# Float64 weights in two VectorE steps behind a ScalarE step, small masks in PSUM, and a new order, in a fused attention and two-layer kernel

## The chip, the cores and the metric

The kernel runs on one core of one Trainium2 chip, in one launch. The metric is device time in microseconds (us) of that core. A program written in Python builds the whole instruction stream ahead of time: every engine (TensorE or PE, VectorE or DVE, ScalarE or ACT, GpSimd or POOL, and SyncE or SP, which issues all the transfers) then runs its own list in order, with semaphores between the engines.

## The reference

Three stages follow each other. Attention takes q, k and v in float32 (2 batches, 8 heads, 768 positions, 64 wide); each query and key is assigned to the nearest of 16 centroids of its head, and only pairs with the same cluster count. Then come two dense layers on 1536 tokens, 512 to 2048 to 512 wide, with float64 weights:

```python
q_assign = np.argmax(np.einsum('bhsd,hcd->bhsc', q_n, c_n), axis=-1)
k_assign = np.argmax(np.einsum('bhsd,hcd->bhsc', k_n, c_n), axis=-1)
mask = q_assign[:, :, :, None] == k_assign[:, :, None, :]
scores = np.where(mask, scale * np.matmul(q, k.transpose(0, 1, 3, 2)), -1000000000.0)
attn = np.exp(scores - np.max(scores, axis=-1, keepdims=True))
attn = attn / (np.sum(attn, axis=-1, keepdims=True) + 1e-09)
x = np.matmul(attn, v)            # heads side by side: 1536 x 512
h = x @ w_in;  x2 = (h * np.cos(h)) @ w_out                         # layer 1
h = x2 @ w_in; out = (h * (1.0 / (1.0 + np.exp(-h)))) @ w_out       # layer 2, other weights
```

## The kernel before

Every matrix product is made of three f16 products: each operand is scaled by a power of two and split into a high part (the value rounded to f16) and a low part (the rest). So nearly every piece of data goes through a rounding to f16 (ScalarE as a rule) and a subtraction (GpSimd or VectorE) before TensorE can use it.

**Weights.** Each of the four weight matrices is loaded in 16 pieces of 128 by 512 float64, as pairs of 32-bit words, into a buffer of 4 KB a partition (`conv`, load on line 692). VectorE builds the float32 bit pattern from the upper word by shifts and masks (L698 and L701, or L704 and L706) and ors in the upper bits of the lower word (L713 or L716). In 20 of the 64 pieces (`LOW`: 8 of the first w_in, 4 of each other matrix) the third step is instead a ScalarE conversion of the lower word (L710) and an addition on GpSimd (L711). `VIA` says for which matrices the half-made word lies in one of three PSUM buffers (`p_pb`, which the scores and the layer-1 products use too): all but layer 2's w_out. A sum over the weights follows, on TensorE (`gram`) for layer 1 and on ScalarE (L438) for layer 2, then a power-of-two scale and the split into high and low (`split`, L753 or L754, L737 to L741, L765).

**Attention.** K and V of a pair of heads are loaded, scaled, split and transposed (`prep_kv`); Q likewise for two blocks of 128 queries (`prep_q`). `clusters` finds the largest of 16 products with centroids by five small VectorE steps (L548 to L556) and writes the cluster's mask into extra columns, so that a wrong cluster lowers the score. `attention` takes a block of 128 queries, head by head in order: scores on TensorE (L905), the row maximum on VectorE (L915), exponentials on ScalarE (L934) with their sum, rounding (L941 on ScalarE or L943 on VectorE), the low part on GpSimd (L948), a transposing DMA (L514), and the product with V (L958). At the end of a block the sums are inverted (L967 to L969), the result is scaled, split and transposed into `xT`.

**Layers.** `layer1_in` (L1034 to L1036) and `layer1_out` (L1092 to L1094) run for units of one or two blocks, mixed with the attention of later units. After the last attention the right half of the memory is reused for layer 2's weights; `layer2` (from L1113) then runs in three parts of 512 tokens.

**Order.** No order is written by hand. Each step is a task with an engine, a planned duration, dependences, buffers and a priority; `Graph.run` plays the plan forward and takes, on each engine, the ready task with the lowest priority number whose buffers are free. The instruction streams are issued in that planned order. The table `T` holds the offsets of the priorities and, for tasks that may run on either of two engines (`alt`), a handicap in planned microseconds for the second. `DLAT` is the planned latency of a transposing DMA beyond its length.

Of the kernel before, what the change touches and what calls it, by code (L numbers as in the profile page):

```python
# [21 lines left out]
T = dict(PW_IN=-684337, PW_OUT=-449, PW_STEP=418, W_AHEAD=-1995, KV0=823, KSTEP0=-2590, V0=926, Q0=-836, KSTEP=558, PREP=-1693,  # L22
         PREPQ=1972, LD=-1140, LOB=0.16, WB=-2.45, HB=0.96, EB=10.85, KB=-9.17, GB=2.58, CB=0.17, XB=-0.43, SB=1.07, L2B=-1018,
         PV=-1572, HI=16965, LO=957, XP=2026, G1=3179, GE=531, GC=1965, G2=4172, GO=147, W2=-641, XD=94557, TB=7.8, WH=-0.35,
         GATE=0)
UNITS = [(0, 0, 1), (0, 1, 1), (0, 2, 2), (0, 4, 2), (1, 0, 2), (1, 2, 2), (1, 4, 2)]

LOW = (2,1,1,1)
# [90 lines left out]
class Graph:  # L119
# [9 lines left out]
    def add(self, eng, dur, fn, deps=(), pri=0.0, acq=(), use=(), lat=0.0, table=None, alt=None, port=False):  # L129

        opts = {eng: (dur, fn, 0.0)}
        if alt:
            opts[alt[0]] = (alt[1], alt[2], alt[3])
# [103 lines left out]
def dve(cols, fast=False):  # L237
    return 0.069 + cols / (1920 if fast else 960)
# [30 lines left out]
DLAT, LLAT, SLAT = 1.18, 1.7, 0.3  # L269


def fused_kernel(tc, q, k, v, cent, w1i, w1o, w2i, w2o, out, dbg=None):
# [4 lines left out]
    P = 128  # L277
# [24 lines left out]
    with tc.manual_schedule(), tc.tile_pool(name="dram", bufs=1, space=DRAM) as dpool:  # L302
# [45 lines left out]
        ohb = rsb([P, 4 * NT * NC + 8 * NT], F16, "ohb")  # L348
# [179 lines left out]
        def clusters(nb, stacks, rhs, dst, dep, pr, use, psum_use):  # L528
# [29 lines left out]
            t = add("DVE", 3 * dve(nb * NC) + 0.17, f_o2, [t], pr, use=[oh], port=True)  # L558
# [23 lines left out]
        def prep_kv(b, hp, pr):  # L582
# [17 lines left out]
                      [sc], pr, acq=[nk], use=[kf, ring])  # L600
            lo_k = lo_task(hk, lambda: nk.ap[:, :, :, 0:64], lambda: kf.ap, lambda: c(2), n, [h_k], [nk, kf, ring], pr, PRE[0][b])
            c_k = add("DVE", dve(n / 2, True), lambda: DV.tensor_copy(na.ap[:, :, :, 32:96], hk()), [h_k], pr + 5, acq=[na], use=[nk],
                      alt=("ACT", act(n), lambda: AC.activation(out=na.ap[:, :, :, 32:96], in_=hk(), func=AF.Copy), T["CB"]), port=True)
# [23 lines left out]
            t = add("ACT", act(n, SCL), lambda: AC.activation(out=vb.ap[:, 0], in_=vf.ap, func=AF.Copy, scale=vs), [t], pr, acq=[vb], use=[vf])  # L627
# [4 lines left out]
        def prep_q(b, t, pr):  # L632
# [3 lines left out]
            if t % 2 == 0:  # L636
# [8 lines left out]
                sg_t = add("DVE", 0.13, lambda: DV.tensor_scalar(  # L645
# [8 lines left out]
                      [sc], pr, acq=[nq], use=[qf2, ring])  # L654
            lo_q = lo_task(hq, lambda: nq.ap[:, 0, :, 64:128], qv, lambda: c(2), n, [h_q], [nq, qf2, ring], pr, PRE[1][b])
            c_q = add("DVE", dve(n / 2, True), lambda: DV.tensor_copy(nq.ap[:, 1, :, 32:96], hq()), [h_q], pr + 5, use=[nq],
                      alt=("ACT", act(n), lambda: AC.activation(out=nq.ap[:, 1, :, 32:96], in_=hq(), func=AF.Copy), T["CB"]), port=True)
# [12 lines left out]
        def x_scale(b):  # L670

            m, xi, fac = col(), col(), col(NPAIR)
# [3 lines left out]
            def f():  # L676
                DV.tensor_reduce(out=m, in_=sv[b], axis=AX.X, op=ALU.min)
                DV.tensor_reduce(out=xi, in_=svi[b], axis=AX.X, op=ALU.max)
                DV.tensor_scalar(fac, svi[b], m, None, op0=ALU.mult)
# [5 lines left out]
        def conv(dst, acc, src, shape3, pri, dst_buf=None, pool=None, deps=(), dst_deps=(), add_low=False, via=False):  # L685
# [5 lines left out]
            d = lambda: dst().bitcast(I32)  # L691
            l = add("SP", dma(P * WC * 8), lambda: SP.dma_start(out=wi(), in_=src), deps, pri - T["W_AHEAD"], acq=[w], lat=LLAT)
            ex = [dst_buf] if dst_buf else []
            if via:

                mb = Buf(p_pb)
                m = lambda: mb.ap[:, :WC].bitcast(I32)
                a = add("DVE", dve(WC), lambda: DV.tensor_scalar(  # L698
                    m(), word(1), 3, 0x3FFFFFFF, op0=ALU.logical_shift_left, op1=ALU.bitwise_and), [l], pri, acq=[mb], use=[w])
                to, td, tu = (d, dst_deps, ex) if add_low else (m, (), [])  # L700
                b_ = add("DVE", dve(WC), lambda: DV.scalar_tensor_tensor(  # L701
                    to(), word(1), -0x40000000, m(), op0=ALU.bitwise_and, op1=ALU.bitwise_or), [a, *td], pri - 1, acq=tu, use=[w, mb])
            else:
                a = add("DVE", dve(WC, True), lambda: DV.tensor_scalar(  # L704
                    d(), word(1), 3, 0x3FFFFFFF, op0=ALU.logical_shift_left, op1=ALU.bitwise_and), [l, *dst_deps], pri, acq=ex, use=[w], port=True)
                b_ = add("DVE", dve(WC), lambda: DV.scalar_tensor_tensor(  # L706
                    d(), word(1), -0x40000000, d(), op0=ALU.bitwise_and, op1=ALU.bitwise_or), [a], pri - 1, use=[w, *ex], port=True)
            if add_low:

# [627 lines left out]
```

## Time and profile before

| | us |
|---|---|
| three timed runs | 802.25, 803.54, 804.64 |
| median | 803.54 |
| the profiled execution, its own time | 802.85 |
| its span, first to last instruction | 800.5 |
| busy in it: PE, DVE, ACT, POOL | 711.9, 533.2, 493.5, 282.9 |

The span is what the profile sees; the own time of the same execution holds 2.35 us more around it. Busy times are unions over an engine's instructions, so an engine that is never idle has the whole stretch as its busy time. Durations of single instructions overlap with their neighbours on the same engine.

### The profile page before, as it was taken

Reading aid. Unit: us, or ns where it says so; the run is one execution under the profiler, and the core shown is the slowest. Engines: PE = TensorE matmul, PEld = TensorE weight load, DVE = VectorE, ACT = ScalarE, POOL = GpSimd, SP = SyncE. Lnnn points to the kernel's source line nnn. Section 1 sums busy time; section 2 is a strip of 40 time slices with the busy share of each in tenths; the row PEclk is TensorE's granted clock in tenths of the full one; section 3 lists DMA queues with packets and bytes.
Section 4 is the critical chain, followed back from the end, with each engine's and each line's share of the span. In section 5 each row is a group of like instructions: output and inputs, shape, how many; then the busy total and the mean of one; then the engine's idle time right before and its main releaser. Section 6 shows DMA issues by size and latency. Waiting matters only on the chain.

```text
span 800.5 us, 16869 instructions
## 1 busy us (share of the span) xinstructions
PE 711.9 (89%) x6745; PEld 485.4 (61%) x6745; DVE 533.2 (67%) x1151; ACT 493.5 (62%) x773; POOL 282.9 (35%) x240
## 2 busy tenths in 40 slices
PE   2468777988978998999999999999899999999998
PEld 1344354867956977877887888884344444444443
DVE  7899798697778798798688757787970155015400
ACT  4658676798888898889678755555671254015400
POOL 3242455367676366557458532241020000000000
PEclk9999689999998999999999999999999999999999
DMA  8944399969999999979969965432041000000000
GB/s 305 330 158 133 85 206 208 210 113 211 184 200 193 248 186 189 188 162 209 206 141 193 194 200 202 145 119 67 27 137 73 27 1 0 27 27 1 0 27 26
DMA packets 233902, 111.29 MB, mean 139 GB/s; under 512 B 199520, under 2 KB 221536, under 8 KB 233824
## 3 DMA queue, kind: packets, MB, share of 16 engines
q1 hardware_dynamic: 233824, 110.23, 62.0%
q8 instruction: 52, 0.85, 0.4%
q14 instruction: 26, 0.21, 0.1%
HBM read 50.36 MB, written 10.49 MB: 76 GB/s over the span
## 4 chain that ended last, share of the span: by engine, by line
PE 52%; DVE 19%; DMA 14%; issue 6%; ACT 4%; POOL 4%; SPq 0%; POOLq 0%; DVEq 0%; ACTq 0%
DMA gen<-gen 8%; PE pb L1217 4%; PE pb L1219 4%; PE pb L1218 4%; DMA ws<-in_moe_w_in_dram 4%; PE pb L905 4%; PE xn_ps L958 3%; POOL gen L948 3%; PE pb L1034 3%; PE pb L1036 3%; PE pb L1035 3%; PE xn_ps L1254 3%; PE xn_ps L1252 3%; PE xn_ps L1253 3%; PE g_ps L1254 3%
## 5 line engine op out<-in xcount | busy, mean ns | idle before, releaser
L948 POOL TENSOR_TENSOR gen<-e,gen 128x768 f16<-128x768 f32 x96 | 159.2, 1671 | 64.2 <-ACT gen L941 34.8
L1034 PE MATMUL pb<-xT,w 128*128 128x256 f16 (+1 forms) x448 | 110.8, 260 | 4.6 <-DVE cols L443 4.6
L1036 PE MATMUL pb<-xT,w 128*128 128x256 f16 (+1 forms) x448 | 111.0, 260 | 0.0
L1035 PE MATMUL pb<-xT,w 128*128 128x256 f16 (+1 forms) x448 | 110.8, 260 | 0.0
L934 ACT ACTIVATE e<-pb,small 128x768 f32<-128x768 f32 x96 | 94.6, 988 | 26.3 <-DVE small L919 10.8
L1093 PE MATMUL g_ps<-gT,w 128*128 128x256 f16 (+1 forms) x448 | 109.7, 257 | 0.7 <-POOL gT L1058 0.7
L1094 PE MATMUL g_ps<-gT,w 128*128 128x256 f16 (+1 forms) x448 | 109.8, 257 | 0.0
L1092 PE MATMUL g_ps<-gT,w 128*128 128x256 f16 (+1 forms) x448 | 109.7, 257 | 0.0
L915 DVE TENSOR_REDUCE small<-pb 128x1 f32<-128x768 f32 x96 | 89.7, 950 | 12.6 <-PE pb L905 12.3
L905 PE MATMUL pb<-kst,qst 96*128 96x512 f16 (+3 forms) x384 | 79.4, 339 | 10.6 <-DVE w L713 2.6
L958 PE MATMUL xn_ps<-vst,gen 128*128 128x64 f16 x1728 | 67.8, 196 | 21.3 <-DMA gen<-gen 21.3
L958 PEld LDWEIGHTS <-gen 128*128 128x128 f16 x1728 | 62.1, 100 | 34.9 <-DMA gen<-gen 30.7
L1058 POOL TENSOR_TENSOR gT<-e,gT 128x768 f16<-128x768 f32 (+2 forms) x36 | 54.7, 1529 | 77.3 <-ACT gT L1057 55.2
L1217 PE MATMUL pb<-x2T,w 128*128 128x512 f16 x192 | 73.4, 382 | 2.6 <-DVE e L1233 2.6
L1219 PE MATMUL pb<-x2T,w 128*128 128x512 f16 x192 | 73.5, 383 | 0.0
L1218 PE MATMUL pb<-x2T,w 128*128 128x512 f16 x192 | 73.4, 382 | 0.0
L941 ACT ACTIVATE gen<-e 128x768 f16<-128x768 f32 x86 | 71.0, 839 | 1.2 <-PE xn_ps L958 0.9
L1233 DVE SCALAR_TENSOR_TENSOR e<-e,pb 128x512 f32<-128x512 f32 x48 | 32.9, 685 | 57.8 <-ACT e L1231 57.7
L1237 DVE SCALAR_TENSOR_TENSOR w<-e,w 128x512 f16<-128x512 f32 x48 | 33.5, 700 | 50.2 <-PE pb L1219 27.1
L905 PEld LDWEIGHTS <-qst 128*128 128x128 f16 (+1 forms) x384 | 36.7, 101 | 34.1 <-issue 16.6
L1092 PEld LDWEIGHTS <-w 128*128 128x128 f16 x448 | 43.7, 98 | 9.6 <-issue 1.7
L1035 PEld LDWEIGHTS <-w 128*128 128x128 f16 x448 | 44.3, 99 | 8.5 <-issue 4.9
(201 smaller groups left out, 1520.7 us busy)
## 6 DMA issues: line engine op xcount, KB each, us to landing
ws<-in_moe_w_out_dram SPq DMA_DIRECT2D x24, 512.0 KB, 4.6
gT<-in_moe_w_in_dram SPq DMA_DIRECT2D x16, 512.0 KB, 4.8
ws<-in_moe_w_in_dram SPq DMA_DIRECT2D x16, 512.0 KB, 4.1
xT<-in_moe_w_out_dram SPq DMA_DIRECT2D x8, 512.0 KB, 4.8
w_dram<-x2s SPq DMA_DIRECT2D x16, 256.0 KB, 2.8
st<-w_dram SPq DMA_DIRECT2D x8, 512.0 KB, 3.5
stq<-in_q_dram SPq DMA_DIRECT2D x6, 512.0 KB, 5.0
gen<-in_k_dram SPq DMA_DIRECT2D x8, 384.0 KB, 5.3
```

The source lines that it names most:

```text
L905: PE.matmul(out=sbk.ap[:, c0:c1], lhsT=qs.ap[:kk, a, h], rhs=kb.ap[:kk, a, j].rearrange("p t c -> p (t c)")[:, c0:c1], start=(a == 1), sto ...
L948: tl = add("POOL", pool2(S), lambda hi=hi, lo=lo, ex=ex: PO.tensor_tensor(lo(), ex(), hi(), op=ALU.subtract), [th], pr + T["LO"], use=[*eu ...
L958: PE.matmul(out=o, lhsT=hb.ap[:, pi, kt], rhs=vb.ap[:, vi, j, kt], start=(kt == 0 and pi == 0 and vi == 0), stop=(kt == NT - 1 and pi == 1 ...
L1034: PE.matmul(out=o, lhsT=wh[:, d, fs], rhs=xb.ap[:, 0, d, :n], start=(d == 0), stop=False)
L1035: PE.matmul(out=o, lhsT=wh[:, d, fs], rhs=xb.ap[:, 1, d, :n], start=False, stop=False)
L1036: PE.matmul(out=o, lhsT=wl[:, d, fs], rhs=xb.ap[:, 0, d, :n], start=False, stop=(d == ND - 1))
L1092: PE.matmul(out=o, lhsT=wh, rhs=gh, start=(f == 0 and i == 0), stop=False, skip_group_check=True)
L1093: PE.matmul(out=o, lhsT=wh, rhs=gl, start=False, stop=False, skip_group_check=True)
L1094: PE.matmul(out=o, lhsT=wl, rhs=gh, start=False, stop=(f == NF - 1), skip_group_check=True)
L1217: PE.matmul(out=o, lhsT=wh[:, d, fs], rhs=x[:, 0, d], start=(d == 0), stop=False)
L1218: PE.matmul(out=o, lhsT=wh[:, d, fs], rhs=x[:, 1, d], start=False, stop=False)
L1219: PE.matmul(out=o, lhsT=wl[:, d, fs], rhs=x[:, 0, d], start=False, stop=(d == ND - 1))
```

## The change

- `conv` has one form for all 64 pieces. ScalarE turns the lower word into a float32 near -2 whose lowest mantissa bits are the lower word's upper bits and whose top bits are set; VectorE shifts the upper word and ors it in; VectorE puts the top two bits right with an or and an and. The half-made word lies in PSUM where `VIA` says so, else in place of the lower word. `LOW` is gone.
- `clusters` writes its masks as float32 into unused columns of the same PSUM buffer instead of f16 in memory.
- The roundings of K, V, Q and their copies, of the exponentials and of layer 1's result may run on any of three engines, each with its own handicap.
- The sums of a block are prepared on GpSimd (two steps) and inverted on VectorE; one scale of Q's moves to GpSimd; the maxima of layer 1's result are kept in one array and reduced once.
- `DLAT` goes from 1.18 to 2.24, and every number of `T` is new, so that the order of all tasks differs. Layer 1's w_in keeps a priority far in front; K and V of the last two head pairs now come before it (`KSTEP0`), and the loads of weights are moved in front of where they stood (`W_AHEAD`).

```diff
-T = dict(PW_IN=-684337, PW_OUT=-449, PW_STEP=418, W_AHEAD=-1995, KV0=823, KSTEP0=-2590, V0=926, Q0=-836, KSTEP=558, PREP=-1693,
...
+T = dict(PW_IN=-4283839, PW_OUT=-527, PW_STEP=702, W_AHEAD=1200, KV0=-1591, KSTEP0=-2793319, V0=4033, Q0=-668, KSTEP=313,
...
-LOW = (2,1,1,1)
...
-DLAT, LLAT, SLAT = 1.18, 1.7, 0.3
+DLAT, LLAT, SLAT = 2.24, 1.7, 0.3
...
-                DV.tensor_tensor(e2(), e1(), io, op=ALU.mult)
-                DV.tensor_reduce(out=m2(), in_=e2(), axis=AX.X, op=ALU.max)
-                DV.tensor_tensor(e1(), io, m2().to_broadcast(bc), op=ALU.is_equal)
+                DV.tensor_tensor(pv(2), pv(1), io, op=ALU.mult)
+                DV.tensor_reduce(out=m2(), in_=pv(2), axis=AX.X, op=ALU.max)
+                DV.tensor_tensor(e1(), pv(2), m2().to_broadcast(bc), op=ALU.is_equal)
...
             h_k = add("ACT", act(n, SCL), lambda: AC.activation(out=hk(), in_=kf.ap, func=AF.Copy, scale=c(2)),
-                      [sc], pr, acq=[nk], use=[kf, ring])
+                      [sc], pr, acq=[nk], use=[kf, ring],
+                      alt=[("POOL", pool1(n), lambda: PO.tensor_scalar(hk(), kf.ap, c(2), 1.0, op0=ALU.mult, op1=ALU.mult), T["KP"]),
+                              ("DVE", dve(n, True), lambda: DV.tensor_scalar(hk(), kf.ap, c(2), None, op0=ALU.mult), T["KD"])], port=True)
...
-                a = add("DVE", dve(WC), lambda: DV.tensor_scalar(
-                    m(), word(1), 3, 0x3FFFFFFF, op0=ALU.logical_shift_left, op1=ALU.bitwise_and), [l], pri, acq=[mb], use=[w])
...
-                r_ = add("ACT", act(WC, SRC), lambda: AC.activation(out=word(0), in_=word(0).bitcast(U32), func=AF.Copy, scale=2.0 ** -29), [l], pri - 2, use=[w])
-                c_ = add("POOL", pool2(WC) + 0.11, lambda: PO.tensor_tensor(d(), d(), word(0), op=ALU.add), [b_, r_], pri - 2, use=[w, *ex])
...
+            mb = Buf(p_pb) if via else None
+            mu = [mb] if via else []
+            m = lambda: (mb.ap[:, :WC].bitcast(I32) if via else word(0))
+
+            r_ = add("ACT", act(WC, SRC), lambda: AC.activation(out=m().bitcast(F32), in_=word(0).bitcast(U32), func=AF.Copy,
+                                                                scale=-0.93 * 2.0 ** -51, bias=-2.0), [l], pri, acq=mu, use=[w])
+            a = add("DVE", dve(WC), lambda: DV.scalar_tensor_tensor(
+                m(), word(1), 3, m(), op0=ALU.logical_shift_left, op1=ALU.bitwise_or), [r_, *dst_deps], pri - 1, use=[w, *mu], port=not via)
+            c_ = add("DVE", dve(WC), lambda: DV.scalar_tensor_tensor(
+                dst().bitcast(I32), word(1), 0x3FFFFFFF, m(), op0=ALU.bitwise_or, op1=ALU.bitwise_and), [a], pri - 2,
+                acq=ex, use=[w, *mu], port=not via)
...
-                    s8, r8 = su.ap[:, 0:H], su.ap[:, H:2 * H]
-                    DV.tensor_scalar(s8, s8, 1e-9 * 2.0 ** 14, None, op0=ALU.add)
-                    DV.reciprocal(r8, s8)
...
-                tr = add("DVE", 0.52, f_r, [*tes, xs_task[b]], pr, use=[su], port=True)
+                    s8 = su.ap[:, 0:H]
+                    PO.tensor_scalar(s8, s8, 1e-9 * 2.0 ** 14, 1.0, op0=ALU.add, op1=ALU.mult)
+                    PO.tensor_tensor(s8, s8, cfac[b], op=ALU.mult)
+
+                tr = add("POOL", 0.4, f_r, [*tes, xs_task[b]], pr, use=[su])
+                tr = add("DVE", 0.12, lambda su=su: DV.reciprocal(su.ap[:, H:2 * H], su.ap[:, 0:H]), [tr], pr, use=[su])
```

## Rows read from the trace of the kernel before

**Rows 1.** The page's slices of 20 us: TensorE's busy tenths.

```profile
PE   2468777988978998999999999999899999999998
```

**Rows 2.** Busy time by stretch, four stretches of the whole span.

```profile
core 0: us, PE busy (x) PEld busy (x) DVE busy (x) ACT busy (x) POOL busy (x), PEclk, DMA share, GB/s
0.00:145.00 145.00, 92.03 (x819) 56.75 (x820) 123.20 (x322) 96.43 (x139) 60.08 (x87) 0.92 0.76 205
145.00:460.00 315.00, 288.93 (x4035) 244.23 (x4032) 255.99 (x584) 259.94 (x422) 187.90 (x129) 0.98 1.02 188
460.00:543.00 83.00, 79.92 (x746) 71.36 (x745) 59.68 (x97) 44.70 (x77) 24.16 (x18) 1.00 0.52 162
543.00:800.50 257.50, 251.02 (x1156) 113.05 (x1154) 94.33 (x149) 92.39 (x136) 10.79 (x8) 0.99 0.10 34
```

**Rows 3.** Busy time by stretch, the opening in three parts, same columns.

```profile
0.00:40.00 40.00, 13.05 (x110) 9.36 (x110) 32.97 (x80) 22.74 (x32) 12.46 (x43) 1.00 0.94 317
40.00:82.00 42.00, 30.91 (x265) 19.74 (x266) 40.34 (x106) 29.26 (x35) 13.04 (x14) 0.99 0.46 152
82.00:145.00 63.00, 48.07 (x445) 27.65 (x444) 49.89 (x138) 44.43 (x72) 34.59 (x31) 0.82 0.84 170
```

**Rows 4.** The chain of waits, 0 to 82 us: start, us, what.

```profile
18.71 1.20 DVE pb L698 x2
19.90 1.19 DVE pb L701 x2
...
21.60 0.68 DVE w L713
...
32.65 6.89 DMA gT<-in_moe_w_in_dram
```

**Rows 5.** Groups by line, whole span: the conversion of the first w_in.

```profile
L698 DVE TENSOR_SCALAR pb<-gT 128x512 int32<-128x512 int32 x16 | 11.0, 691 | 3.3 <-DMA gT<-in_moe_w_in_dram 3.2
...
L711 POOL TENSOR_TENSOR w<-w,gT 128x512 int32<-128x512 int32 x8 | 10.2, 1286 | 17.0 <-DVE w L701 15.1 <-issue 1.9
...
L713 DVE SCALAR_TENSOR_TENSOR w<-gT,pb 128x512 int32<-128x512 int32 x8 | 5.3, 678 | 0.0
L710 ACT ACTIVATE gT<-gT 128x512 int32<-128x512 uint32 x8 | 5.3, 676 | 5.0 <-DMA gT<-in_moe_w_in_dram 5.0
```

**Rows 6.** The chain of waits, 82 to 150 us.

```profile
131.61 6.49 DMA gen<-gen
...
145.79 0.06 PE pb L1034
```

**Rows 7.** Transfers by line: issues, KB each, median us to landing.

```profile
gen<-in_k_dram SPq DMA_DIRECT2D x8, 384.0 KB, 5.3
```

**Rows 8.** Groups by line, VectorE, 100 to 150 us: the small mask steps.

```profile
L549 DVE TENSOR_TENSOR ohb<-pb,ohb 128x128 f16<-128x128 f32 x1 | 0.3, 291 | 0.0
L556 DVE TENSOR_TENSOR ohb<-iota,ohb 128x128 f16<-128x128 f16 x1 | 0.3, 291 | 0.0
...
L554 DVE TENSOR_TENSOR ohb<-ohb,iota 128x128 f16<-128x128 f16 x1 | 0.2, 206 | 0.0
```

**Rows 9.** Groups by line, VectorE, 145 to 460 us.

```profile
L706 DVE SCALAR_TENSOR_TENSOR x2s<-ws,x2s 128x512 int32<-128x512 int32 x14 | 9.6, 688 | 0.2
L716 DVE SCALAR_TENSOR_TENSOR x2s<-ws,x2s 128x512 int32<-128x512 int32 x10 | 9.4, 940 | 0.1
...
L556 DVE TENSOR_TENSOR ohb<-iota,ohb 128x128 f16<-128x128 f16 (+1 forms) x13 | 6.9, 529 | 0.4
L704 DVE TENSOR_SCALAR x2s<-ws 128x512 int32<-128x512 int32 x14 | 6.8, 485 | 0.6 <-DMA ws<-in_moe_w_out_dram 0.6
...
L969 DVE TENSOR_TENSOR small<-small,cols 128x8 f32<-128x8 f32 x10 | 5.3, 529 | 0.3
...
L554 DVE TENSOR_TENSOR ohb<-ohb,iota 128x128 f16<-128x128 f16 (+1 forms) x13 | 4.7, 365 | 0.1
L967 DVE TENSOR_SCALAR small<-small 128x8 f32<-128x8 f32 x10 | 4.6, 458 | 2.9 <-ACT e L934 2.8
```

**Rows 10.** Who waited for whom, TensorE, 145 to 543 us: us, times, longest.

```profile
PE xn_ps L958 <- DMA gen<-gen: 16.3, 18, 1.6
```

More of the change, by code (lines that the diff above doesn't have):

```diff
@@ L131, in add @@
         opts = {eng: (dur, fn, 0.0)}
-        if alt:
-            opts[alt[0]] = (alt[1], alt[2], alt[3])
+        for a in alt if isinstance(alt, list) else [alt] if alt else []:
+            opts[a[0]] = (a[1], a[2], a[3])
         t = Task(opts, deps, pri, list(acq), use, lat, table, port)
@@ L626, in prep_kv @@
             sready[b, hp] = t
-            t = add("ACT", act(n, SCL), lambda: AC.activation(out=vb.ap[:, 0], in_=vf.ap, func=AF.Copy, scale=vs), [t], pr, acq=[vb], use=[vf])
+            t = add("ACT", act(n, SCL), lambda: AC.activation(out=vb.ap[:, 0], in_=vf.ap, func=AF.Copy, scale=vs), [t], pr, acq=[vb], use=[vf],
+                    alt=[("POOL", pool1(n), lambda: PO.tensor_scalar(vb.ap[:, 0], vf.ap, vs, 1.0, op0=ALU.mult, op1=ALU.mult), T["KP"]),
+                              ("DVE", dve(n, True), lambda: DV.tensor_scalar(vb.ap[:, 0], vf.ap, vs, None, op0=ALU.mult), T["KD"])], port=True)
             vready[b, hp] = lo_task(lambda: vb.ap[:, 0], lambda: vb.ap[:, 1], lambda: vf.ap, lambda: vs, n, [t], [vb, vf], pr, PRE[2][b])
@@ L676, in f, with conv @@
             def f():
-                DV.tensor_reduce(out=m, in_=sv[b], axis=AX.X, op=ALU.min)
                 DV.tensor_reduce(out=xi, in_=svi[b], axis=AX.X, op=ALU.max)
-                DV.tensor_scalar(fac, svi[b], m, None, op0=ALU.mult)
+                for j in range(2):
+                    DV.tensor_scalar(fac.rearrange("p (a b) -> p a b", b=2)[:, :, j], sv[b], xi, None, op0=ALU.mult)
             u = next(i for i, x in enumerate(UNITS) if x[0] == b)
             xs_task[b] = add("DVE", 0.3, f, [sready[b, hp] for hp in range(NPAIR)], u * 1000)
-        def conv(dst, acc, src, shape3, pri, dst_buf=None, pool=None, deps=(), dst_deps=(), add_low=False, via=False):
+        def conv(dst, acc, src, shape3, pri, dst_buf=None, pool=None, deps=(), dst_deps=(), via=False):
             w = Buf(pool or p_ws)
@@ L1056, in layer1_in @@
                     r(), r(), FG, ph(), op0=ALU.mult, op1=ALU.mult), [t], e, use=[rb, hb])
[L1057 removed]
+                t = add("ACT", act(N4), lambda r=r, sl=sl: AC.activation(out=gb.ap[:, 0, sl], in_=r(), func=AF.Copy), [t, *(g_free if u == 0 else [])], e + T["GC"], acq=[gb], use=[rb],
+                        alt=[("DVE", dve(N4, True), lambda r=r, sl=sl: DV.tensor_copy(gb.ap[:, 0, sl], r()), T["GD"]),
+                             ("POOL", pool1(N4), lambda r=r, sl=sl: PO.tensor_scalar(gb.ap[:, 0, sl], r(), 1.0, 1.0, op0=ALU.mult, op1=ALU.mult), T["GP"])], port=True)
                 gready[u].append(add("POOL", pool2(N4), lambda r=r, sl=sl: PO.tensor_tensor(
@@ L1177, in layer2 @@
                 tl = add("SP", dma(P * 8192), lambda lo_t=lo_t, hi_t=hi_t: SP.dma_start(out=l2["xf"], in_=x2_dram[:, :, lo_t * P:hi_t * P]),
-                         [t_swap, *[t for u in us for t in x2done[u][1:]]], pr, acq=[xfb], lat=LLAT)
+                         [t_swap, *[t for u in us for t in x2done[u][1]]], pr, acq=[xfb], lat=LLAT)
                 m, am2, sx, ix, ths, ofac, wk2 = col(), col(), col(), col(), [col(), col()], col(), col(3)
-                def f_m(us=us, m=m):
-                    DV.tensor_copy(m, x2max[us[0]])
-                    for u in us[1:]:
-                        DV.tensor_tensor(m, m, x2max[u], op=ALU.max)
-                t = add("DVE", 0.4, f_m, [x2done[u][0] for u in us], pr)
+                t = add("DVE", 0.1, lambda us=us, m=m: DV.tensor_reduce(out=m, in_=x2mx[:, 2 * us[0]:2 * us[-1] + 2], axis=AX.X, op=ALU.max),
+                        [t for u in us for t in x2done[u][0]], pr)
                 t, mb, mps = all_max(lambda m=m: m, [t], pr)
```

74 lines of the change are left out of this document (27 added, 47 removed).

## The prediction

> **What bounds the kernel now.** I read the page's slices first, then the busy time by stretch, then the chain of waits of the opening, then the groups by line. The slices show TensorE nearly full from the eighth slice (140 us) on and far from full before it [rows 1]. The stretches put numbers on it: from 543 us to the end TensorE is busy 251.02 of 257.5 us, from 460 to 543 it is busy 79.92 of 83, from 145 to 460 it is busy 288.93 of 315 (26.1 idle), but from 0 to 145 only 92.03, so 53 us idle [rows 2]. The last two stretches can give back almost nothing, whatever VectorE and ScalarE do there; the opening can give most, the middle at most 26.
>
> In the opening VectorE is busy 32.97 of 40, 40.34 of 42 and 49.89 of 63 us [rows 3]. The chain of waits of 0 to 82 us runs along it, mostly through the weight conversion: L698, L701, L713 stand on it in turn, each step worth about 0.60 us there (1.20 for two) although one alone lasts 0.69, because the next one starts before the last has ended [rows 4, 5]. Loads of w_in stand on it three times, the longest 6.89 us [rows 4], so in the first 40 us (317 GB/s [rows 3]) the transfers are a second bound close behind. From 82 us, where the first scores start, the chain goes through TensorE's own work, VectorE, ScalarE, GpSimd and a transposing DMA (6.49 us), and reaches layer 1 at 145.8 us [rows 6]. So the forecast is for one stretch, 0 to 145, with a smaller term for the middle.
>
> **The conversion.** Before, 44 of the 64 pieces take three VectorE steps; 20 (8 of the 16 of the first w_in, 4 of 16 in each other matrix) take two, a ScalarE step and a GpSimd addition. After, all take one ScalarE step and two VectorE steps. In the opening lie all 32 pieces of the layer-1 weights: 20 of them (8 + 12) lose one VectorE step, the L713 one. By busy time that is 20 × 0.68 = 13.6 us [rows 5], by the chain's spacing 20 × 0.60 = 12.0 us [rows 4]. VectorE's opening goes from 123.2 us to 109.6 [rows 2]. The other 12 pieces lose 12 × 1.29 = 15.5 us of GpSimd [rows 5], which was busy 60 of 145 us and so is worth nothing in itself. ScalarE gets 20 more steps. The row of its conversion from memory to memory is 0.676 us [rows 5]; the new one writes PSUM, which no row shows, and I take the same: +13.5 us. ScalarE's opening goes from 96.4 us to 109.9 [rows 2], level with VectorE. So the gain is bounded below by 0 (ScalarE's added steps take the place of the removed ones) and above by 13.6; since the two then run beside each other, with 35 us of room each in 145, I take 12.0. The cover of the ScalarE steps is that room; where it fails, see the third rival. The added wait, VectorE's first step for ScalarE, queues VectorE's later instructions behind a ScalarE queue that holds exponentials and roundings; the PSUM buffer is held from the ScalarE step on, some 0.7 us longer, and scores wait for one of the same three buffers.
>
> **The new order of the opening.** K and V of the last two head pairs get priorities below the first w_in's, so four loads of 384 KB go down the SP queue ahead of all weights. That is 1.57 MB, at the 317 GB/s of [rows 3] 5.0 us by which the first weight lands later. VectorE has the norms of those heads to do meanwhile, and the same four loads stood between the weight loads before, so the bounds are 0 and +5.0; I take +2. The other K, V and Q loads, which one after another took 5.3 us in the median to land [rows 7], go ahead of w_out. The scores of a block are issued head by head from head 0, whose K comes last in both orders, so early K of the last heads starts no score earlier.
>
> **VectorE's small steps in PSUM.** In the quiet stretch around 100 to 150 us the masks of 128 columns take 206 ns (L554, memory to memory), 291 (L556, the same) and 291 (L549, reading PSUM) [rows 8]; in the middle, where GpSimd is busy 60% of the time, L554 and L556 average 365 and 529 [rows 9]. With PSUM operands nearest L549's row, 13 instances in the middle save 13 × (0.365 + 0.529 - 2 × 0.291) = 4.1 us of VectorE. [...]
>
> **The middle, 145 to 460.** The conversions of the second w_out stay in SBUF: 14 of them cost 14 × (0.485 + 0.688) + 10 × 0.940 = 25.8 us [rows 9], and become 28 × 0.69 = 19.3, so 6.5 less VectorE and 10 × 0.67 = 6.7 more ScalarE. Of the normalisation (L967 to L969) two steps of 0.458 and 0.529 go to GpSimd, ten times: 9.9 us [rows 9]. In return the reciprocal, the scaling and the transpose behind it wait for a GpSimd queue of long subtractions; the cover is layer 1's matmuls of the unit before, and without it each is late by one such subtraction. VectorE sheds 6.5 + 4.1 + 9.9 = 20.5 of 256 us, at ScalarE's +6.7 on 260 [rows 2], which the free choice of engine for f16 roundings can spread. But TensorE sets this stretch. Its largest named wait is for the transposed exponentials, 16.3 us [rows 10], which no lighter VectorE shortens; the order may, since the planner's assumed latency of a transpose rises from 1.18 to 2.24 us, and it places the matmuls behind them by that. Bounds: a gain of 26.1 (all idle time) and a loss of the same size as the wait, 16.3, if the new order doubles it. I take a gain of 6, a quarter of the idle time, nearer to the stretch's 92% busy than to either end.
>
> **The rest.** The second w_in (12 pieces, 8.2 us less VectorE) and the maxima lie between 460 and 560 us, where TensorE has 3.1 us idle to 543 [rows 2]: 0, covered by the layer-1 matmuls of the last units; without that cover the steps would be worth 12 × 0.60 = 7.2.
>
> **Sum.** -12.0 + 2 - 6 + 0 = -16. The profiled execution took 802.85 us (span 800.5, 2.35 around it), so 786.9; the median of the runs shown, 803.54, is 0.7 above it. Forecast 787, own range 779 to 797.
>
> **Rivals.** (1) *More than that: TensorE's clock comes back as well.* The granted clock from 82 to 145 us is 0.82 of full [rows 3], and before it TensorE was busy only 30.91 of 42 us. [...] Eye matmuls and scores do stand on the chain there. [...] Against it: nothing in the change adds TensorE work early. (2) *The relief stays off the path.* In the first 40 us transfers, later ScalarE, take over the chain as soon as VectorE recedes. For it: the 6.89 us load [rows 4] and ScalarE's 109.9 against VectorE's 109.6. Then only a part of the 12.0 is kept, and the +2 and a middle without gain remain: 797 to 805; with none of it, no change. (3) *Slower: ScalarE becomes the bound of the opening.* The conversion now begins on ScalarE, in order behind exponentials, splits and K roundings; if these cannot move to other engines its 13.5 us come onto the path while VectorE's 12 stay unpaid. It decides once ScalarE's busy time in the opening passes the 123 us that VectorE needed. Half of the added time on the path and the +2 give 802.85 + 6.7 + 2 = 811.6, all of it 818. Against it: 109.9 is 13 us short of that point, if the roundings do not move the other way.
>
> **Chances.** 0.43 for the forecast, 0.18 for rival 1, 0.02 for still less, 0.20 for rival 2, 0.17 for rival 3. A difference of 0.3% (2.4 us) is about what a measurement of this kernel can tell from none; of rival 2's chance 0.09 lies inside it and 0.11 below. Faster 0.43 + 0.18 + 0.02 + 0.11 = 0.74, same 0.09, slower 0.17. For 8 in 10 the range reaches through most of rival 1 and to the lower end of rival 3, which begins where no change ends, at 805: 768 to 808, with some 0.05 left out below and 0.12 above.
>
> **What would show it.** Right: layer 1's first matmul some 10 us earlier than 145.8; VectorE near 110 us busy before it and no third conversion step; ScalarE near 110; TensorE's idle time in the middle near 20; the stretch from the first layer-2 matmul to the end 257 as before. Wrong: ScalarE or a load where VectorE stood on the opening's chain (rival 2 or 3), longer waits of L958 for the transposes, a later first conversion by more than 5 us, or a layer 2 that waits for its weights.

## The result and the profile after

The changed kernel takes 792.03 us in the median of 4 runs (790.49 to 793.23), the kernel before 802.89 beside it (4 runs, 801.3 to 804.64): a ratio of 0.9863, with a 95% interval of 0.9834 to 0.9892, so 10.9 us faster. Its profiled execution took 791.40 us, with a span of 789.5.

The busy time by stretch of the kernel after, in the stretches of [rows 2, 3] up to 460 us:

```profile
core 0: us, PE busy (x) PEld busy (x) DVE busy (x) ACT busy (x) POOL busy (x), PEclk, DMA share, GB/s
0.00:40.00 40.00, 14.08 (x117) 10.10 (x118) 31.32 (x78) 23.40 (x35) 2.70 (x35) 1.00 0.94 326
40.00:82.00 42.00, 31.74 (x285) 18.88 (x284) 38.71 (x111) 33.62 (x42) 20.30 (x22) 0.92 0.53 175
82.00:145.00 63.00, 50.40 (x582) 34.86 (x582) 52.59 (x120) 44.41 (x75) 35.78 (x32) 0.81 0.88 167
145.00:460.00 315.00, 292.89 (x3974) 246.12 (x3971) 262.92 (x577) 235.06 (x390) 204.12 (x161) 0.98 1.01 189
```

In the middle VectorE and ScalarE have changed places: ScalarE fell from 259.94 us [rows 2] to 235.06, VectorE rose from 255.99 to 262.92, although by the prediction's sum the change takes some 20 us of steps off VectorE there.

Stretches at fixed times cut the two kernels at different places of their work. So both were also cut at their own landmarks: the first matmul of layer 1, the last score, the first matmul of layer 2, the end. The kernel before:

```profile
0.00:145.60 145.60, 92.62 (x834) 57.35 (x835) 123.20 (x322) 97.03 (x140) 60.68 (x87) 0.92 0.76 205
145.60:444.20 298.60, 272.89 (x3773) 229.83 (x3771) 245.01 (x569) 247.39 (x405) 178.07 (x124) 0.98 1.01 187
444.20:543.00 98.80, 95.36 (x989) 85.16 (x988) 70.66 (x113) 56.64 (x94) 33.39 (x24) 1.00 0.62 169
```

The last stretch is that of [rows 2]. The kernel after:

```profile
0.00:131.30 131.30, 82.93 (x734) 51.52 (x735) 110.73 (x283) 92.58 (x138) 49.27 (x79) 0.89 0.77 218
131.30:434.50 303.20, 280.68 (x3853) 235.04 (x3851) 258.85 (x579) 228.38 (x378) 197.02 (x160) 0.97 1.01 188
434.50:530.70 96.20, 95.35 (x1007) 85.90 (x1006) 63.45 (x97) 63.02 (x108) 37.58 (x27) 1.00 0.65 175
530.70:789.50 258.80, 249.92 (x1157) 112.84 (x1155) 94.11 (x151) 87.86 (x129) 15.99 (x11) 1.00 0.10 34
```

Layer 1 starts 14.3 us earlier. But 100 matmuls (834 against 734) that stood ahead of it now stand behind it, and TensorE's busy time there fell by 9.7 us; only 4.6 of the 14.3 is idle time gone. **A landmark moves with the order of the work; work that moves across it adds nothing to TensorE's idle time**, and TensorE runs all but one tenth of the span. So everything below is counted in idle time (each stretch less its PE busy time):

| us of TensorE idle | before | after | difference |
|---|---|---|---|
| to the first matmul of layer 1 | 53.0 | 48.4 | -4.6 |
| from there to the last score | 25.7 | 22.5 | -3.2 |
| from there to the first matmul of layer 2 | 3.4 | 0.9 | -2.6 |
| from there to the end | 6.5 | 8.9 | +2.4 |
| sum | 88.6 | 80.6 | -8.0 |
| TensorE busy, 6745 matmuls in both | 711.9 | 708.9 | -3.0 |

Together that is the 11.0 us by which the span is shorter. The busy time of the same 1157 matmuls of layer 2 lay between 249.92 and 252.77 us in the kernel after and those below that share its order, so 3.0 us of busy time is not put down to the change. Idle time varies from one execution to the next as well. The program of the kernel after was measured a second time (under `V0`, below), and its profiled execution had 84.0 us of idle time, 3.4 more, with 2.6 us less busy time. Its stretch from the first matmul of layer 1 to the last score:

```profile
129.50:431.90 302.40, 277.38 (x3853) 233.20 (x3852) 260.35 (x579) 228.33 (x378) 197.49 (x160) 0.99 1.02 189
```

That is 25.0 us idle instead of 22.5, at a granted clock of 0.99 instead of 0.97. Ahead of layer 1 it had 49.0 instead of 48.4. So the 4 to 5 us won in the opening stand; of the 3.2 in the middle as little as 0.7 may be left.

The chain of waits of the kernel after, in two parts of its opening (start, us, what):

```profile
2.65 8.40 DMA stq<-in_q_dram
...
25.63 7.16 DMA gen<-in_k_dram
```

```profile
49.47 0.55 ACT pb L703
50.04 0.70 DVE pb L705
...
52.27 1.20 ACT pb L703 x2
...
54.40 1.19 DVE gT L707 x2
...
62.59 1.01 ACT w L733
...
64.42 1.34 ACT kst L523
```

The third VectorE step is gone from it. In its place ScalarE stands on the chain, with the new conversion step (L703) itself and with the roundings and copies that queue beside it, and the loads of Q and K stand where a load of w_in stood [rows 4].

The conversion of the first w_in, groups by line of the kernel after, beside [rows 5]:

```profile
L703 ACT ACTIVATE pb<-gT 128x512 f32<-128x512 uint32 x16 | 10.0, 625 | 10.6 <-DMA gT<-in_moe_w_in_dram 7.8 <-DVE cols L441 1.8 <-DVE w L707 0.9
L705 DVE SCALAR_TENSOR_TENSOR pb<-gT,pb 128x512 int32<-128x512 int32 x16 | 11.1, 691 | 5.4 <-ACT pb L703 5.2
L707 DVE SCALAR_TENSOR_TENSOR w<-gT,pb 128x512 int32<-128x512 int32 x16 | 10.9, 680 | 0.3
```

VectorE now waits 5.2 us for ScalarE's step. Two groups show what the free choice of an engine did with f16 roundings of exponentials (the kernel after, whole span); before, 10 of the 96 were on VectorE:

```profile
L935 DVE CAST gen<-e 128x768 f16<-128x768 f32 x56 | 42.0, 760 | 2.0 <-ACT e L926 2.0
L933 ACT ACTIVATE gen<-e 128x768 f16<-128x768 f32 x40 | 33.4, 838 | 1.9 <-DMA gen<-gen 0.9 <-ACT e L926 0.8
```

And who waited for whom, TensorE from 145 to 543 us of the kernel after, the row that answers to [rows 10] and the two behind it:

```profile
PE xn_ps L951 <- DMA gen<-gen: 6.9, 6, 3.5
PE pb L897 <- ACT e L926: 4.4, 8, 1.6
PE pb L897 <- DVE ohb L554: 3.6, 5, 1.0
```

The wait for the transposes is 9.4 us shorter, but the scores (L897) now wait more: for the exponentials 4.4 us instead of 1.0, for a step of the masks 3.6 instead of 0.6.

### The profile page after: what moved, and what is told of

Read it like the earlier page. It is cut to its first block, busy times and chain, and to the rows that moved or that the text cites. A ratio compares the mean times of both kernels' runs of the same rounds, so it can differ in the third digit from the quotient of the medians.

```text
span 789.5 us, 16836 instructions
## 1 busy us (share of the span) xinstructions
PE 708.9 (90%) x6745; PEld 485.3 (61%) x6745; DVE 527.1 (67%) x1107; ACT 471.8 (60%) x752; POOL 299.9 (38%) x276
## 4 chain that ended last, share of the span: by engine, by line
PE 61%; DVE 20%; ACT 7%; DMA 6%; issue 4%; POOL 1%; SPq 1%; DVEq 0%; ACTq 0%; POOLq 0%
PE pb L1205 5%; PE pb L1206 5%; PE pb L1204 5%; DVE small L907 4%; PE pb L1026 4%; PE pb L1027 4%; PE xn_ps L951 4%; PE pb L1028 4%; PE pb L897 4%; PE g_ps L1084 3%; PE g_ps L1085 3%; PE xn_ps L1241 3%; PE g_ps L1241 3%; PE xn_ps L1240 3%; PE g_ps L1240 3%
## 5 line engine op out<-in xcount | busy, mean ns | idle before, releaser
L941 POOL TENSOR_TENSOR gen<-e,gen 128x768 f16<-128x768 f32 x96 | 162.3, 1702 | 63.0 <-DVE gen L935 34.6
L1084 PE MATMUL g_ps<-gT,w 128*128 128x256 f16 (+1 forms) x448 | 109.6, 257 | 1.1 <-ACT x2s L1091 1.1
L1086 PE MATMUL g_ps<-gT,w 128*128 128x256 f16 (+1 forms) x448 | 109.6, 257 | 0.0
L897 PE MATMUL pb<-kst,qst 96*128 96x512 f16 (+3 forms) x384 | 80.8, 344 | 22.1 <-ACT e L926 12.0
L951 PEld LDWEIGHTS <-gen 128*128 128x128 f16 x1728 | 63.1, 100 | 15.9 <-DMA gen<-gen 10.9
L897 PEld LDWEIGHTS <-qst 128*128 128x128 f16 (+1 forms) x384 | 37.3, 101 | 47.5 <-issue 29.9
L1222 ACT ACTIVATE w<-e 128x512 f16<-128x512 f32 x48 | 30.1, 628 | 32.7 <-DVE e L1220 32.7
L1224 DVE SCALAR_TENSOR_TENSOR w<-e,w 128x512 f16<-128x512 f32 x48 | 33.3, 699 | 23.4 <-ACT w L1222 23.0
```

The lines of the kernel that those rows point to most:

```text
L897: PE.matmul(out=sbk.ap[:, c0:c1], lhsT=qs.ap[:kk, a, h], rhs=kb.ap[:kk, a, j].rearrange("p t c -> p (t c)")[:, c0:c1], start=(a == 1), sto ...
L941: tl = add("POOL", pool2(S), lambda hi=hi, lo=lo, ex=ex: PO.tensor_tensor(lo(), ex(), hi(), op=ALU.subtract), [th], pr + T["LO"], use=[*eu ...
L951: PE.matmul(out=o, lhsT=hb.ap[:, pi, kt], rhs=vb.ap[:, vi, j, kt], start=(kt == 0 and pi == 0 and vi == 0), stop=(kt == NT - 1 and pi == 1 ...
L1084: PE.matmul(out=o, lhsT=wh, rhs=gh, start=(f == 0 and i == 0), stop=False, skip_group_check=True)
```

## The experiments

Every kernel was timed against the kernel before. Kernels are compared with the kernel after by the difference of the two ratios times 802.5 us, and by TensorE's idle time of the profiled execution (span less PE busy). The second measurement of the kernel after gave 793.01 us, a ratio of 0.9899 (0.9864 to 0.9933), 2.9 us above the first. So a difference of up to 3 us in the times isn't told from none; where two numbers stand, the one in brackets is against the second measurement. "Same order" means that the order of all instructions on every engine is the one of the kernel after; where it isn't said, the planner made a new one for the edited tasks.

### One cost put back or doubled, same order

**The old conversion in 20 pieces of layer 1.** These are the pieces that lost a step. The ScalarE step goes, its slot and the next two hold the three old VectorE steps:

```diff
-AC.activation(out=m().bitcast(F32), in_=word(0).bitcast(U32), func=AF.Copy, scale=-0.93 * 2.0 ** -51, bias=-2.0)
+DV.tensor_scalar(m(), word(1), 3, 0x3FFFFFFF, op0=ALU.logical_shift_left, op1=ALU.bitwise_and)
-DV.scalar_tensor_tensor(m(), word(1), 3, m(), op0=ALU.logical_shift_left, op1=ALU.bitwise_or)
+DV.scalar_tensor_tensor(m(), word(1), -0x40000000, m(), op0=ALU.bitwise_and, op1=ALU.bitwise_or)
-DV.scalar_tensor_tensor(dst().bitcast(I32), word(1), 0x3FFFFFFF, m(), op0=ALU.bitwise_or, op1=ALU.bitwise_and)
+DV.scalar_tensor_tensor(dst().bitcast(I32), word(0), 29, m(), op0=ALU.logical_shift_right, op1=ALU.bitwise_or)
```

> The kernel after with every task and buffer in its place in the order; only in the 20 pieces of the layer-1 weights that lost a VectorE step the old three VectorE steps are issued in the slots of the new three (the ScalarE step is gone there). Theory A (the removed VectorE step sets the opening's time): 20 x 0.60 = 12 us come back, about 804 us, level with the kernel before. Theory B (the new order gives the gain, the step lies beside other work): 790 to 795.

Measured: 801.41 us, ratio 0.9987 (0.9965 to 1.0010), so 10.0 us more than after (7.1) and level with before. Its busy time by stretch, to the first matmul of layer 1 and to the last score:

```profile
0.00:138.40 138.40, 82.88 (x733) 52.02 (x734) 121.82 (x302) 81.52 (x118) 48.04 (x79) 0.91 0.73 206
138.40:444.10 305.70, 281.39 (x3853) 235.81 (x3852) 260.01 (x579) 228.41 (x378) 197.50 (x160) 0.97 1.00 187
```

The same matmuls stand ahead of layer 1 as in the kernel after (733 records and 734), and idle time there is 55.5 us against 48.4: +7.1 (6.5). The middle adds 1.8, which is within what the same program varies by. So the relief of VectorE in the opening is real and, in the new order, is worth most of the gain: rival 2, in which it stays off the path, falls.

**ScalarE's new step twice, in the same 20 pieces.**

```diff
-AC.activation(out=m().bitcast(F32), ...)
+for _ in range(2):
+    AC.activation(out=m().bitcast(F32), ...)
```

> The kernel after, same order, the new ScalarE step issued twice in the same 20 pieces (the second writes the same values): 20 x 0.63 = 12.6 us more ScalarE work in the opening. If ScalarE has room there, as the sum took it: 792 to 795. If ScalarE is the bound of the opening (third rival): 802 to 805.

Measured: 801.82 us, ratio 0.9976 (0.9944 to 1.0008), 9.1 us more than after (6.2), for 20 × 0.63 = 12.6 us of ScalarE. The stretch to layer 1 and a part of the chain of waits of this kernel (L708 is the doubled step):

```profile
0.00:138.40 138.40, 85.51 (x733) 52.26 (x734) 111.36 (x283) 104.96 (x158) 48.40 (x79) 0.90 0.74 207
```

```profile
52.33 0.53 ACT pb L708
52.88 0.64 ACT pb L708
```

ScalarE is busy 104.96 of 138.4 us, so it has 33 us of "room", and yet its added steps land on the chain. Idle time to layer 1 is 52.9 us, 4.5 more than after (3.9). Of the 9.7 us by which the span is longer another 4.7 are TensorE busy time over the whole span (713.6 against 708.9, same matmuls), half of them in the opening; that part isn't told apart from what one execution differs from another. What stands: the cover claimed for ScalarE's steps isn't whole, and of the 12.6 us added 4 to 9 come out.

**GpSimd's work put back.** In the 12 pieces that lost GpSimd's addition, GpSimd adds halves of the finished piece into a tile that nothing reads:

```diff
+PO.tensor_tensor(junk_t, dst().bitcast(I32)[:, 256 * z:256 * z + 256], dst().bitcast(I32)[:, 256 * z:256 * z + 256], op=ALU.add)
```

> The kernel after, same order, with about 12 x 1.3 us of GpSimd additions back behind the conversion of the 12 opening pieces that had lost theirs (into a small tile that nothing reads). As the sum took it, GpSimd's part of the old conversion was worth nothing: 790 to 794. If any extra work in the opening delays the end, whichever engine has it: 799 to 804.

Measured: 795.67 us, ratio 0.9924 (0.9900 to 0.9949), 4.9 us more than after (2.0, with overlapping intervals; the second measurement was taken beside this one). GpSimd is busy 67.6 us instead of 49.3 to layer 1; TensorE's idle time there is 2.3 us longer (1.6). The landmarks moved by 0.6 us at the first matmul of layer 1 and not at all at the last score (434.5) and the first matmul of layer 2 (530.7). So GpSimd's load by itself was worth some 2 us, and that is at the edge of what can be told. The old place of the addition, between VectorE's step and the sum over the weights that waits for it, isn't put back by this edit and isn't tested.

**Less relief in the middle.** The masks back in memory, the two steps of the sums from GpSimd back to VectorE, and VectorE's first conversion step twice in 12 pieces of the second w_out:

```diff
-PO.tensor_scalar(s8, s8, 1e-9 * 2.0 ** 14, 1.0, op0=ALU.add, op1=ALU.mult)
-PO.tensor_tensor(s8, s8, cfac[b], op=ALU.mult)
+DV.tensor_scalar(s8, s8, 1e-9 * 2.0 ** 14, 1.0, op0=ALU.add, op1=ALU.mult)
+DV.tensor_tensor(s8, s8, cfac[b], op=ALU.mult)
...
-DV.tensor_tensor(pv(2), pv(1), io, op=ALU.mult)
+DV.tensor_tensor(e2(), e1(), io, op=ALU.mult)
```

> The kernel after, same order, with the three edits of the middle undone: the clusters' masks in memory as f16, the two steps on the sums on VectorE, and in the 12 pieces of layer 2's w_out that lost a VectorE step the first one issued twice (the second writes the same values). By the sum's working this is some 20 us of VectorE back between 145 and 460 us. If VectorE's relief there was worth the 6 us of the forecast: 797 to 799. If TensorE covers it: 791 to 794.

Measured: 809.50 us, ratio 1.0087 (1.0059 to 1.0116), 18.0 us more than after (15.1). The stretch from the first matmul of layer 1 to the last score:

```profile
134.80:448.70 313.90, 284.32 (x3854) 237.32 (x3853) 282.24 (x608) 228.26 (x378) 192.98 (x140) 0.96 0.99 182
```

VectorE has 23.4 us more to do in it than after (258.85); the stretch is 10.7 us longer, 7.1 of it idle time of TensorE (29.6 against 22.5; 4.6 against the 25.0) and 3.6 busy time at a lower granted clock (0.96 against 0.97), with the same matmuls. Another 3.5 us came ahead of it, where the masks and sums of the first blocks lie. TensorE's idle time over the span is 92.1 us, 11.5 more than after (8.1). So in the new order at least a part of VectorE's relief is on the path of the middle. A group of VectorE from 130 to 450 us of this kernel, one of the two steps on the sums:

```profile
L978 DVE TENSOR_TENSOR small<-small,cols 128x8 f32<-128x8 f32 x10 | 7.1, 713 | 0.3
```

**The masks alone back in memory.** The diff is the mask part of the one above.

> The kernel after, same order, only the clusters' masks back in memory as f16. By the rows (the memory-to-memory step at 717 ns against 312 in PSUM in the middle, 14 times, the last one at 378 against 310): 14 x 0.47 = 6.6 us more VectorE, so a third of what undoing all three edits of the middle cost, 796 to 800. [...]

Measured: 794.60 us, ratio 0.9893 (0.9860 to 0.9926), 2.4 us more than after with overlapping intervals (0.5 less than the second measurement), so no difference is shown in the end. The steps differ. VectorE from 130 to 450 us, this kernel and then the kernel after:

```profile
L553 DVE TENSOR_TENSOR ohb<-ohb,iota 128x128 f16<-128x128 f16 (+1 forms) x14 | 10.1, 718 | 0.1
L555 DVE TENSOR_TENSOR ohb<-iota,ohb 128x128 f16<-128x128 f16 (+1 forms) x14 | 7.4, 532 | 0.5
```

```profile
L552 DVE TENSOR_TENSOR pb<-pb,iota 128x128 f32<-128x128 f32 (+1 forms) x14 | 4.4, 312 | 0.1
L554 DVE TENSOR_TENSOR ohb<-pb,ohb 128x128 f16<-128x128 f32 (+1 forms) x14 | 4.3, 310 | 0.8
```

17.5 against 8.7 us: in this order PSUM saves 8.8 us of VectorE. In the kernel before the same two steps averaged 365 and 529 ns [rows 9]: there the planner starts them only when GpSimd's planned instruction is over (`port=True` on their task), and the kernel after, which this run shares its order with, does not. So 8.8 us is the price of memory in an order made without that care.

That so much VectorE time is worth so little in the end has a reason in the trace. The masks lie in a PSUM buffer that the scores need too, and hold it until their last step. TensorE's wait for that step, in the kernel after to 531 us and then with the masks in memory to 534, where the buffer is free after the second step (L548):

```profile
PE pb L897 <- DVE ohb L554: 7.1, 7, 2.6
```

```profile
PE pb L898 <- DVE ohb L548: 1.3, 1, 1.3
```

So VectorE's busy time alone doesn't price a step here: 8.8 of the 23.4 us of the experiment before cost at most a few us, and the rest of its 15 to 18 lies with the sums' steps and the doubled conversion steps, which were not told apart.

**Old conversion in 12 pieces of layer 2's w_in.** The diff is the first one, in the calls of layer 2 (`n % 4 >= 1`).

> The kernel after, same order, with the old three VectorE steps in the 12 pieces of layer 2's w_in that had lost one (no ScalarE step in these). The sum took 0, covered by the last layer-1 matmuls: 791 to 793. If the conversion after 460 us is on the path: up to 12 x 0.60 = 7 more, 799.

Measured: 794.98 us, ratio 0.9905 (0.9876 to 0.9934): 3.4 us more than after (0.5), intervals overlapping. The last score (434.2) and the first matmul of layer 2 (530.7) stay where they were. So no cost is shown, and the sum's 0 isn't refuted.

### Half of the change, with a new plan

**The conversion alone**, in the kernel before (its `T` and `DLAT` kept), and **the new `T` and `DLAT` alone**, in the kernel before:

```diff
-LOW = (2,1,1,1)
...
+            r_ = add("ACT", act(WC, SRC), lambda: AC.activation(out=m().bitcast(F32), in_=word(0).bitcast(U32), func=AF.Copy,
...
```

> The kernel before with the new conversion alone; priorities, planned transpose latency and all else as before, the plan made anew. Theory A: 12 us less in the opening, 789 to 795. Theory B: most of the gain missing, 798 to 803. A new plan can move the time by itself, by an amount that no run has shown yet.

```diff
-T = dict(PW_IN=-684337, ...)
+T = dict(PW_IN=-4283839, ...)
-DLAT, LLAT, SLAT = 1.18, 1.7, 0.3
+DLAT, LLAT, SLAT = 2.24, 1.7, 0.3
```

> The kernel before with the new table of priorities and handicaps and the planned transpose latency of 2.24, the old conversion and all other steps as before (one number, V0, stays 926, since the plan does not close with the new one). Theory A: the order's own share of the forecast, -6 + 2 = -4, so 796 to 802. Theory B: the order carries the gain, 789 to 794.

Measured: 830.61 us, ratio 1.0347 (1.0298 to 1.0396), and 828.97 us, ratio 1.0343 (1.0274 to 1.0413). Both halves lose 28 us where the whole gains 11.

**All of the change but the numbers of `T` and `DLAT`:**

```diff
-T = dict(PW_IN=-4283839, ...)
+T = dict(PW_IN=-684337, ...)
-DLAT, LLAT, SLAT = 2.24, 1.7, 0.3
+DLAT, LLAT, SLAT = 1.18, 1.7, 0.3
```

> The kernel after with the old table of priorities and handicaps (the new keys keep their values) and the planned transpose latency of 1.18, the plan made anew. If a plan is only as good as the fit of its table to its set of tasks: 815 to 835, as for the two other half changes. If the new steps carry the gain under any table: 790 to 797.

**`DLAT` alone in the kernel before:**

```diff
-DLAT, LLAT, SLAT = 1.18, 1.7, 0.3
+DLAT, LLAT, SLAT = 2.24, 1.7, 0.3
```

> The kernel before with the planned latency of a transposing DMA at 2.24 instead of 1.18, old table, plan made anew. If the better-fitting latency alone shortens the waits for the transposes (the reason given for the middle's -6): 795 to 800. If the table fits one plan only: 810 to 830.

**One number of `T` in the kernel after:**

```diff
-V0=4033
+V0=926
```

> The kernel after with one priority offset changed (V0, for V's preparation, 926 as before instead of 4033) and the plan made anew; the same work. If a plan is good for many tables, 789 to 795. If the table fits one set of tasks only, as the two runs of 829 and 831 us suggest, 805 to 830.

Measured: 834.37 us, ratio 1.0393 (1.0316 to 1.0469); 824.13 us, ratio 1.0281 (1.0254 to 1.0308); and 793.01 us, ratio 0.9899 (0.9864 to 0.9933).

The last of these is not a different kernel: with the other `V0` the planner arrives at the same instruction streams, instruction for instruction. So it says nothing on how many tables a plan is good for; it is the second measurement of the kernel after that is used above.

The four plans that do differ lose 22 to 32 us against the kernel before. Who waited for whom, TensorE to the start of layer 2, in the kernel with the old numbers (to 543 us) and then in the kernel after (to 531):

```profile
PE xn_ps L951 <- DMA gen<-gen: 25.1, 25, 2.5
PE g_ps L772 <- DVE w L707: 22.3, 12, 7.2
```

```profile
PE g_ps L772 <- DVE w L707: 21.3, 12, 7.3
...
PE xn_ps L951 <- DMA gen<-gen: 7.3, 7, 3.5
```

The waits for transposes are 17.8 us longer with the old numbers; those for converted weights are as long in the kernel after, so they are not what is lost. With `DLAT` alone the waits for transposes fall, from 21.3 us (0 to 543 us) in the kernel before to 14.6, as the reason given for it has it, and yet the kernel is 22 us slower; the scores' waits for exponentials are 12.7 us in it instead of 2.2. So the loss has no single place, and what in the numbers makes it isn't shown. What is shown is that the steps and the order can't be priced one by one by planning anew with numbers chosen for another set of tasks; the prices above are prices inside the new order. Whether numbers chosen anew for each half would do better wasn't tried.

### A version that beats both

Layer 2 is 1.3 us longer after (258.8 against 257.5), with 2.4 us more idle time. One hole is in it; busy time from 600 to 620 us of the kernel after, and who waited for TensorE there:

```profile
600.00:620.00 20.00, 16.85 (x80) 7.55 (x78) 3.51 (x18) 3.56 (x4) 0.00 (x0) 1.00 0.07 27
```

```profile
DVE cols L409 <- PE pb L429: 32.8, 1, 32.8
```

The matmul that spreads the maximum of layer 2's second part over the partitions (L429) stands in TensorE's queue behind the matmuls of the first part; VectorE's reduction waits 32.8 us for it, and what follows it comes late. It gets a lower priority number, so an earlier place:

```diff
-t, mb, mps = all_max(lambda m=m: m, [t], pr)
+t, mb, mps = all_max(lambda m=m: m, [t], pr - 1500)
-t = add("DVE", 0.25, lambda mps=mps, am2=am2: absmax(am2, mps(), AX.X), [t], pr, use=[mb])
+t = add("DVE", 0.25, lambda mps=mps, am2=am2: absmax(am2, mps(), AX.X), [t], pr - 1500, use=[mb])
```

> The kernel after with layer 2's small matmul and reduction for the maximum over the partitions given a priority 1500 lower, so that the one of the second part no longer stands behind the first part's matmuls on TensorE. The trace after shows 3.15 us without TensorE work between 600 and 620 us, VectorE waiting 32.8 us for that matmul. If that is all: 788.5 to 790, 3 us less. If the hole is only moved (the plan changes from 531 us on): 791 to 793.

Measured: 785.37 us in the median of 6 runs (784.21 to 787.71), ratio 0.9803 (0.9781 to 0.9826), 4.8 us less than after (7.7, taken beside each other), intervals apart from both. The same stretch, and layer 2 to the end:

```profile
600.00:620.00 20.00, 20.00 (x94) 9.07 (x93) 1.38 (x2) 3.03 (x5) 0.00 (x0) 1.00 0.07 27
528.50:782.50 254.00, 249.19 (x1156) 112.68 (x1153) 93.42 (x144) 88.03 (x131) 17.27 (x11) 1.00 0.11 36
```

The hole is gone and layer 2 has 4.8 us of idle time instead of 8.9 (9.0), so some 4 us of what was timed is shown in the trace.

## Why the prediction came out as it did

The forecast of 787 lies 5 us under the time, which is inside its own range, and faster was right. Of the 11.0 us by which the span is shorter, 3.0 are busy time of TensorE, for which the prediction has no term; in idle time it was 8.0, half of the 16 forecast. By its own terms:

**The conversion: mechanism right, size off.** It took 12.0 us. Undone in the new order it is 7.1 us of idle time ahead of layer 1 (6.5), and 10.0 by the times (7.1). The step that failed is the cover: "the two then run beside each other, with 35 us of room each". To the first matmul of layer 1 VectorE's busy time came out as forecast (109.6, measured 110.73) and ScalarE's lower (109.9, measured 92.58, since roundings moved off it and layer 1 starts earlier), so there was room. But the room was an average: doubling ScalarE's step leaves 4.5 us of idle time there out of 12.6 added, about what the conversion gave less than forecast. ScalarE's step stands on the chain in front of VectorE's two, and where the piece is urgent the chain pays for all three. Rival 3 had this mechanism and put its point at 123 us of ScalarE; the cost came at 92.6. Only one doubling was run, so whether every added step costs the same isn't shown. The sign named for this term, layer 1 some 10 us earlier, came out (14.3), but mostly because matmuls moved behind it: that was luck.

**The new order of the opening: +2 was near the sum, for a wrong reason.** With the old conversion in the new order idle time ahead of layer 1 is 55.5 us, against 53.0 before: +2.5. This holds all else that changed there too (12 additions off GpSimd, masks, sums, free roundings), so it isn't the price of the order alone. And the loads that the prediction saw go first don't. SyncE's issues of the kernel after (start, us):

```profile
0.79 1.82 SPq L697 DMA_DIRECT2D gT<-in_moe_w_in_dram  x4
2.65 0.66 SPq L643 DMA_DIRECT2D stq<-in_q_dram  x1
7.28 4.63 SPq L697 DMA_DIRECT2D gT<-in_moe_w_in_dram  x4
...
12.43 0.43 SPq L587 DMA_DIRECT2D gen<-in_k_dram  x1
```

Weights still go first. The buffers of K and V are handed out in the order in which their tasks were created, so the last head pairs' low priority can't bring them past the first: K of heads 0 and 1 is loaded first in both kernels, not last as the prediction has it. What costs the 2.5 us wasn't isolated.

**The masks: sign right, because GpSimd runs.** The prediction took 4.1 us of VectorE saved; in the new order's middle it is 8.8. The stretch that it calls quiet isn't: GpSimd is busy 26.82 of the 50 us there, and the two steps in memory that it reads there happened to meet no GpSimd instruction. Clear of GpSimd, memory was even the quicker place for one step of the two: the multiplication of 128 columns took 206 to 224 ns in memory in the kernel before, and 289 to 299 in PSUM in the kernel after; the comparison took 291 to 294 and 290 to 292. But over the middle, with GpSimd running, the means in the new order are 718 and 532 ns in memory against 312 and 310. What the prediction had no term for is the PSUM buffer that the masks hold: 7.1 us of waiting scores against 1.3.

**The middle: sign right, size half or less, reason wrong.** It took -6; to the last score idle time fell by 3.2 us, or 0.7 by the second measurement. The wait for transposes did fall, from 16.3 [rows 10] to 6.9, but the scores' waits grew in its place. And the prediction held that "no lighter VectorE shortens" it and left the gain to the order. Taking about 20 us of relief back costs 15 to 18: the new order needs a part of VectorE's relief, and as far as the times tell it isn't the masks' part. The new order has also spent it: 46 more roundings of exponentials run on VectorE, ScalarE lost 24.9 us from 145 to 460 [rows 2], and VectorE ended up with more work there than before. The prediction saw the free choice only as a way to spread ScalarE's 6.7.

**The rest: 0 as a sum.** -2.6 before layer 2 and +2.4 inside it; in layer 2 the matmul for the maximum leaves a hole of 3.15 us, and no step of the prediction looked at it.

**GpSimd's additions:** taken as nothing; their load is worth some 2 us, hardly told from none.

**Rival 1** falls: the granted clock from 82 to 145 us went from 0.82 to 0.81, and from 40 to 82 us from 0.99 [rows 3] to 0.92, although TensorE was a little busier there (31.74 us against 30.91). No run shows a clock that follows TensorE's earlier work, nor what a clock that came back would be worth; over the span the same matmuls were busy 3.0 us less.

## What to carry to other kernels

The busy share of an engine is not room: where two engines hand a piece to each other on the chain, a step moved from one to the other still stands on it, and doubling it in place shows how much. When the order of the work changes too, compare the idle time of the engine that sets the end, stretch by stretch, not the times of landmarks, and measure one program twice to know how far that idle time varies by itself (3.4 us here). Don't price half of such a change with a plan whose numbers were chosen for the other half, and see that an edit to the plan's numbers changes the program at all. Then look for the new order's own holes: one matmul for which VectorE waited 32.8 us was worth almost half as much as all of the change.

## What the runs showed of the hardware

VectorE's multiplication of the masks took 1.57 us in memory where a GpSimd instruction was running when it began, and 0.29 us in PSUM in the same situation. Start and length in us, with the masks in memory, and then in the kernel after:

```profile
143.24 1.64 POOL L1053 TENSOR_TENSOR gT<-e,gT 128x768 f16<-128x768 f32 x1 [2.28 <-ACT gT L1050]
143.39 1.57 DVE L553 TENSOR_TENSOR ohb<-ohb,iota 128x128 f16<-128x128 f16 x1
```

```profile
145.67 1.64 POOL L1052 TENSOR_TENSOR gT<-e,gT 128x768 f16<-128x768 f32 x1 [2.82 <-ACT gT L1049]
145.83 0.29 DVE L552 TENSOR_TENSOR pb<-pb,iota 128x128 f32<-128x128 f32 x1
```

In memory the step ended 0.08 us behind GpSimd's, of which 1.49 us were left when it began. Of its 14 instances from 130 to 450 us eight began under a running GpSimd instruction and took 586 to 1694 ns; the other six took 215 to 258. So the mean of 718 ns is a mixture of the two. The 529 ns of the 128 x 8 step on the sums in the kernel before [rows 9] are one as well: seven of its ten instances took 0.17 us, and three that began under a running GpSimd instruction 1.25 to 1.45. With its first operand and result in PSUM the 14 instances of the multiplication took 289 to 366 ns, GpSimd running or not.

ScalarE's conversion step took 625 ns with its result in PSUM (the group above) and 668 in memory:

```profile
L703 ACT ACTIVATE ws<-ws 128x512 f32<-128x512 uint32 x16 | 10.7, 668 | 0.7 <-DMA ws<-in_moe_w_out_dram 0.7
```

The rows are 43 ns apart. The result in memory also goes to every other word and the one in PSUM does not, and no run here tells the two apart.
